# In every third attention step the next step's score products stand in front of the transposes

## The chip, the cores and the metric

The kernel runs on one core of one Trainium2 chip. The metric is device time in microseconds (us) of one execution. The engines are named as in the profile: PE is TensorE's matmul stream, PEld its weight loads, ACT is ScalarE, DVE is VectorE, POOL is GpSimd and SP the queue that issues most DMAs.

## The reference

The program computes an attention with a hash mask and then two dense feed-forward layers:

```
q_bits, k_bits = (q @ proj > 0), (k @ proj > 0)       # 6 bits per row
mask   = bucket(q_bits)[:, None] == bucket(k_bits)[None, :]
scores = where(mask, q @ k.T / sqrt(64), -1e9)
attn   = softmax(scores) ;  x = attn @ v               # 2 x 8 heads, 768 rows, 64 columns
x = (h * sigmoid(1.702 h)) @ w_out,  h = x @ w_in      # 1536 x 512, inner size 2048
y = (h * tanh(softplus(h))) @ w_out2, h = x @ w_in2
```

All inputs are float32. The kernel keeps that precision by splitting each operand into a high and a low part and adding three products.

## The kernel before, in words

Attention comes first, in one loop over steps `i` (line 821). There are 16 heads of 768 rows, and a step is 128 rows of one head, so 96 steps and a few more to drain. Three steps make a group, two groups (six steps) a head. In one step `i`, four kinds of work of different steps stand side by side:

- `qk(i + 1)` (letter Q, line 603): four products on PE of 384 columns each, which write the 128x768 scores of the next step into a PSUM tile `s`, of which there are two. The second two of them add the mask.
- `clamp(i)` (C, line 621) on DVE: the scores go from PSUM to SBUF, with the row's extreme. It is what frees the tile `s`. `expo(i)` (E, line 630) on ACT: the exponential with the row sum; it ends with a short instruction that reads the accumulator.
- `trp(g, t)` (A and B, line 673), twice in a step: three PE transposes put 128 columns of the three probability tiles of group `g` into one PSUM tile `pt`, and ACT casts that tile to `pth` (the high part). `trl` (a and b, line 686): DVE subtracts to get the low part `ptl`, which is the last reader of `pt`. Group `g` is worked on in steps `3g+3` to `3g+5`, so the first transposes of a group read the exponentials of the three steps just before, the last of them that of step `i - 1`.
- `pv` (P and R, line 693): four products with V of what was transposed in the step before, into the PSUM tile `u`. After the last of a group `u_out` (line 705) copies `u` to SBUF on ACT. This happens in the steps with `i % 3 == 0`, behind the exponential.

Letter T stands for the work listed by step in `todo`: loads, preparation of the next heads, normalisation, the first weights of the feed-forward layers. On PE it has two parts. `s2` (lines 501 and 489) computes hash logits with six products into a tile `prep`, at steps `i % 6 == 2`, and DVE reads that tile as `mk`. `norm1` (line 655) transposes row sums into such a tile, at steps `i % 12 == 5`. Both take their tile from the same pool as the transposes:

```
ps_t = es.enter_context(tc.tile_pool(name="ps_t", bufs=3, space=PSUM))   # line 360
ptile = ps_t.tile([P, 512], F32, tag="pt", name="pt")                    # line 674, in trp
pt = ps_t.tile([P, 512], F32, tag="pt", name="prep")                     # line 502, in s2
```

The pool has three tiles, taken in turn. Who takes one waits for the last reader of the tile taken three before: for a `trp` in step `i` that is mostly a subtraction of the step before.

The order in which a step's parts are issued is written by hand, as a string of these letters (line 753), and each engine runs its instructions in that order. The string before is the same for all steps but step 2:

```
ORDER = "ACaBbETQPR"
for op in ORDER if i != 2 else ORDER.replace("TQ", "QT"):    # line 836
```

The feed-forward layers follow (`moe`, line 873). They are about two thirds of the time and are not touched.

Of the kernel before, what the change touches and what calls it, by code (L numbers as in the profile page):

```python
# [41 lines left out]
def lsh_attention_moe_kernel(  # L42
# [291 lines left out]
    def r_in(m, f, k0=0, k1=KD):  # L334
        if k0 == 0:
            pool, tag = mps["h"], f"h{f % 2}"
            if (m, f // 2) == (0, 1):
                pool, tag = (mps["q"], "Y") if f % 2 else (mps["h"], "y0")
            h_t[m, f] = pool.tile([P, CH], F32, tag=tag, name="h")
        h = h_t[m, f]  # L340
        wh, wl = w_t[m, f, 0]
        n = 3 * k0
        for kk in range(k0, k1):
            wk = slice(kk * P, (kk + 1) * P)
            for a, x in ((wh, xr_hi), (wh, xr_lo), (wl, xr_hi)):
                nc.tensor.matmul(  # L346
                    h, a[:, wk], x[:, kk], start=(n == 0), stop=(n == 3 * KD - 1)
                )
                n += 1

    def attention():
        with ExitStack() as es:
# [67 lines left out]
            def keep_warm(n, cols):  # L420
                t = ps_t.tile([P, 512], F32, tag="pt", name="warm")
                for _ in range(n):
                    nc.tensor.matmul(t[:, :cols], ones[:, :P], ones[:, :cols], start=True, stop=True)
# [179 lines left out]
            def qk(i, parts=(0, 1), fs=(0, 1)):  # L603
                n, t = divmod(i, NT)
                kh, qx, qb, kb, _ = opnd[n]
                if 0 in parts and 0 in fs:
                    st_t[i] = ps_s.tile([P, 2, 512], F32, tag="s", name="s")
                s = st_t[i]
                c = slice(t * P, (t + 1) * P)
                both = (qx, kh, True), (qb, kb, False)  # L610
                for a, bb, st in [both[x] for x in parts]:
                    for f in fs:
                        nc.tensor.matmul(  # L613
                            s[:, f, :HS],
                            a[:, c],
                            bb[:, f * HS : (f + 1) * HS],
                            start=st,
                            stop=not st,
                        )

            def clamp(i):
                s = st_t[i]
                sb = pp.tile([P, 2, HS], F32, tag="p", name="p")
                mn = sm.tile([P, 1], F32, tag="mn", name="mn")
                nc.vector.tensor_scalar(  # L625
                    sb, s[:, :, :HS], NEG, None, ALU.min, ALU.min, accum_out=mn
                )
                st_t[i] = (sb, mn)

            def expo(i):  # L630
                sb, mn = st_t.pop(i)
                n, t = divmod(i, NT)
                p = sb.rearrange("p a b -> p (a b)")
                u, h = divmod(n, 2)
                if t == 0 and h == 0:
                    z_t[u] = sm.tile([P, 2 * NT], F32, tag="z", name="z", bufs=2)
                zc = NT * h + t
                nc.scalar.activation(  # L638
                    p,
                    p,  # L640
                    AF.Exp,
                    bias=mn,
                    scale=-1.0,
                    accum_out=z_t[u][:, zc : zc + 1],
                )
                p_t[i] = p
# [26 lines left out]
            def trp(g, t):  # L673
                ptile = ps_t.tile([P, 512], F32, tag="pt", name="pt")
                for j in range(3):
                    nc.tensor.transpose(  # L676
                        ptile[:, j * P : (j + 1) * P],
                        p_t[3 * g + j][:, t * P : (t + 1) * P],
                        ident,
                    )  # L680
                hi = ptp.tile([P, HS], F32R, tag="pth", name="pth")
                lo = ptp.tile([P, HS], F32R, tag="ptl", name="ptl")
                nc.scalar.copy(hi, ptile[:, :HS])  # L683
                pt_t[g, t] = (hi, lo, ptile)

            def trl(g, t):
                hi, lo, ptile = pt_t[g, t]
                nc.vector.tensor_sub(lo, ptile[:, :HS], rnd(hi))  # L688
                if t == NT - 1:
                    for j in range(3):  # L690
                        p_t.pop(3 * g + j)

            def pv(g, t):
                n, f = divmod(g, 2)
                hi, lo, _ = pt_t.pop((g, t))
                if t == 0:
                    u_t[g] = ps_u.tile([P, 512], F32, tag="u", name="u")
                ut = u_t[g]
                vv = opnd[n][4][0]
                nc.tensor.matmul(ut[:, :HS], vv[:, t, :], hi, start=(t == 0), stop=False)  # L700
                nc.tensor.matmul(ut[:, :HS], vv[:, t, :], lo, start=False, stop=(t == NT - 1))  # L701
                if t == NT - 1:
                    u_out(g)
# [47 lines left out]
            second[2]()  # L751
            LAG = 3
            ORDER = "ACaBbETQPR"
            NZ = 5
            NZL = 2
            PVLAG = LAG + 1
# [2 lines left out]
            def at(step, f, *args):  # L759
                todo.setdefault(step, []).append((f, args))  # L760
# [30 lines left out]
            for u in range(NHD // 2):  # L791
                zs = 2 * NT * (u + 1)
                nz = NZ if u < NHD // 2 - 1 else NZL
                at(zs + 1, norm0, u)
# [26 lines left out]
            for i in range(NSTEP + PVLAG):  # L821
                if i == NSTEP:
                    es_s.close()
                    mps["h"] = ctx.enter_context(
                        tc.tile_pool(name="ps_h", bufs=1, space=PSUM, side="right")
                    )
                parts = iter(range(max(0, 2 * (i - NSTEP)), min(2 * (i - NSTEP) + 2, 2 * KD)))
                for part in parts:
                    r_in(0, part // KD, part % KD, part % KD + 1)
                    break  # L830
                kk = i - LAG
                tr = 0 <= kk < NSTEP
                g, j = divmod(kk, 3)
                kv = i - PVLAG
                gv, jv = divmod(kv, 3)
                for op in ORDER if i != 2 else ORDER.replace("TQ", "QT"):
                    if op == "A" and tr:
                        trp(g, 2 * j)
                    elif op == "B" and tr:
                        trp(g, 2 * j + 1)  # L840
                    elif op == "a" and tr:
                        trl(g, 2 * j)
                    elif op == "b" and tr:
                        trl(g, 2 * j + 1)
                    elif op == "C" and i < NSTEP:
                        clamp(i)
                        if i == 3:
                            second[7]()
                    elif op == "E" and i < NSTEP:
                        expo(i)  # L850
                    elif op == "Q" and i + 1 < NSTEP:
                        qk(i + 1, (0, 1) if i else (1,))
                        if i == 0:
                            keep_warm(4, 256)
                    elif op == "P" and 0 <= kv < NSTEP:
                        pv(gv, 2 * jv)
                    elif op == "R" and 0 <= kv < NSTEP:
                        pv(gv, 2 * jv + 1)
                    elif op == "T":
                        while todo and min(todo) <= i:  # L860
                            st = min(todo)
                            f, args = todo[st].pop(0)
                            if not todo[st]:
                                del todo[st]
                            f(*args)
                for part in parts:
                    r_in(0, part // KD, part % KD, part % KD + 1)
# [5 lines left out]
    def moe():  # L873
        with ExitStack() as es:
# [354 lines left out]
            while due:  # L1229
                flush()  # L1230

    attention()
    moe()

# [53 lines left out]
```

## Time and profile before

| | us |
|---|---|
| median of 3 runs | 730.86 (730.52 to 731.77) |
| the profiled execution | 731.06 |
| its span, first to last instruction | 729.3 |
| PE busy | 723.5 (99%) |
| PEld busy | 631.5 (87%) |
| DVE busy | 616.3 (85%) |
| ACT busy | 469.0 (64%) |
| POOL busy | 185.4 (25%) |

The span is one execution, on the profiler's clock; the execution took 1.8 us more than its span. Busy times are sums over attention and feed-forward alike. PE's clock was granted in full nearly throughout (mean 0.999).

### The profile page before, as it was taken

How to read it: one execution, taken by the hardware profiler on the slowest of the kernel's cores; microseconds unless marked ns; L12 is line 12 of the kernel's file. 1: busy time of each engine (PE TensorE's matmuls, PEld its weight loads, DVE VectorE, ACT ScalarE, POOL GpSimd, SP SyncE). 2: the span in 40 equal slices, each digit the busy share in tenths (PEclk: the TensorE clock that was granted, in tenths of full speed). 3: DMA queues.
4: the chain of work that ended last, by engine and by line, in shares of the span. 5: the costliest groups of instructions: out<-in, count | busy, mean ns of one | idle time of the engine just before them, and what ended most of it. 6: DMA issues, size and time to landing. Idle time of an engine off the chain costs nothing.

```text
span 729.3 us, 11137 instructions
## 1 busy us (share of the span) xinstructions
PE 723.5 (99%) x3856; PEld 631.5 (87%) x3856; DVE 616.3 (85%) x1134; ACT 469.0 (64%) x957; POOL 185.4 (25%) x187
## 2 busy tenths in 40 slices
PE   8999999999999999999999999999999999999998
PEld 6999999999998788888888888888888888888886
DVE  8888889989888959878878797998699899897864
ACT  7888888888898765536546465576635656455340
POOL 7968877889893000000000000000000000000000
PEclk9999999999999999999999999999999999999999
DMA  5745656666624221121211221301302121211004
GB/s 157 199 125 145 190 141 163 182 157 153 170 85 118 109 70 48 58 87 64 82 58 58 88 88 60 112 0 59 115 0 87 59 75 69 88 58 58 1 1 173
DMA packets 25992, 69.53 MB, mean 95 GB/s; under 512 B 4464, under 2 KB 6992, under 8 KB 25936
## 3 DMA queue, kind: packets, MB, share of 16 engines
q1 hardware_dynamic: 25632, 68.62, 31.7%
q8 instruction: 30, 0.49, 0.3%
q10 hardware_dynamic: 304, 0.20, 0.1%
q14 instruction: 26, 0.21, 0.1%
HBM read 49.09 MB, written 3.19 MB: 72 GB/s over the span
## 4 chain that ended last, share of the span: by engine, by line
PE 94%; DVE 2%; ACT 2%; DMA 0%; issue 0%; DVEq 0%
PE y L947 36%; PE X L1010 11%; PE s L613 9%; PE pt L676 9%; PE Y L1010 8%; PE W L1010 7%; PE u L701 4%; PE u L700 4%; PE h L346 4%; PE prep L493 2%; ACT p L638 1%; DMA qn<-in_qt_dram 0%; ACT pth L683 0%; DVE gl L907 0%; DVE Y L1031 0%
## 5 line engine op out<-in xcount | busy, mean ns | idle before, releaser
L688 DVE TENSOR_TENSOR ptl<-pt,pth 128x384 fp32r<-128x384 f32 x192 | 98.1, 553 | 22.4 <-ACT pth L683 20.2
L683 ACT CAST pth<-pt 128x384 fp32r<-128x384 f32 x192 | 82.8, 484 | 28.7 <-PE pt L676 28.7
L638 ACT ACTIVATE p<-p,mn 128x768 f32<-128x768 f32 x96 | 91.2, 950 | 1.7 <-DVE p L625 1.6
L625 DVE TENSOR_SCALAR_CACHE_REDUCE p<-s 128x768 f32<-128x768 f32 x96 | 90.6, 945 | 0.3 <-PE s L613 0.2
L961 DVE TENSOR_TENSOR xq<-xq,y 128x512 f32<-128x512 f32 (+1 forms) x113 | 75.6, 679 | 13.7 <-PE y L947 13.0
L676 PE MATMUL pt<-ident,p 128*128 128x128 f32 x576 | 81.1, 274 | 0.1
L947 PE MATMUL y<-wh,gh 128*128 128x512 f32 (+1 forms) x194 | 75.4, 389 | 0.0
L947 PE MATMUL y<-wl,gh 128*128 128x512 f32 (+1 forms) x194 | 75.4, 389 | 0.0
L947 PE MATMUL y<-wh,gl 128*128 128x512 f32 (+1 forms) x194 | 75.2, 387 | 0.0
L947 PE MATMUL y<-gh,wh 128*128 128x512 f32 x192 | 75.0, 391 | 0.0
L947 PE MATMUL y<-gh,wl 128*128 128x512 f32 x192 | 74.9, 390 | 0.0
L947 PE MATMUL y<-gl,wh 128*128 128x512 f32 x192 | 74.7, 389 | 0.0
L259 ACT CAST wh<-wb 128x512 fp32r<-128x512 f32 x64 | 39.4, 620 | 54.5 <-DVE wb L246 26.2
L676 PEld LDWEIGHTS pt<-ident,p 128*128 128x128 f32 x576 | 68.5, 140 | 6.6 <-ACT p L638 2.4
L700 PE MATMUL u<-pth,vv 128*128 128x384 f32 x192 | 64.7, 337 | 0.0
L701 PE MATMUL u<-ptl,vv 128*128 128x384 f32 x192 | 64.5, 336 | 0.0
L613 PE MATMUL s<-kh,qx 128*128 128x384 f32 x192 | 55.7, 370 | 0.2 <-DVE p L625 0.2
L613 PE MATMUL s<-kb,qb 128*128 128x384 f32 x192 | 49.3, 337 | 0.3 <-POOL qk_m L473 0.2
L261 DVE TENSOR_TENSOR wl<-wb,wh 128x512 fp32r<-128x512 f32 x62 | 42.3, 687 | 3.9 <-ACT wh L259 3.6
L961 DVE TENSOR_TENSOR yr<-yr,y 128x512 f32<-128x512 f32 x56 | 38.2, 684 | 7.8 <-PE y L947 6.9
L947 PEld LDWEIGHTS y<-wh,gl 128*128 128x128 f32 x194 | 36.4, 188 | 7.6
L947 PEld LDWEIGHTS y<-wh,gh 128*128 128x128 f32 x194 | 36.5, 188 | 7.3 <-DVE xq L961 0.4
(272 smaller groups left out, 1842.1 us busy)
## 6 DMA issues: line engine op xcount, KB each, us to landing
raw<-in_wt_dram SPq DMA_DIRECT2D x64, 512.0 KB, 3.6
kn<-in_kt_dram SPq DMA_DIRECT2D x15, 384.0 KB, 4.2
vn<-in_vt_dram SPq DMA_DIRECT2D x8, 384.0 KB, 5.3
ul<-uh SPq DMA_DIRECT2D x16, 192.0 KB
rb<-scr SPq DMA_DIRECT2D x16, 192.0 KB, 3.5
qn<-in_qt_dram SPq DMA_DIRECT2D x15, 192.0 KB, 3.4
qx<-qk_m SPq DMA_DIRECT2D x15, 192.0 KB, 3.9
qb<-qk_m SPq DMA_DIRECT2D x15, 192.0 KB, 5.6
```

The costliest lines, as they stand in the source:

```text
L261: sub(lo, wf, rnd(hi))
L613: nc.tensor.matmul(s[:, f, :HS], a[:, c], bb[:, f * HS : (f + 1) * HS], start=st, stop=not st,)
L625: nc.vector.tensor_scalar(sb, s[:, :, :HS], NEG, None, ALU.min, ALU.min, accum_out=mn)
L638: nc.scalar.activation(p, p, AF.Exp, bias=mn, scale=-1.0, accum_out=z_t[u][:, zc : zc + 1],)
L676: nc.tensor.transpose(ptile[:, j * P : (j + 1) * P], p_t[3 * g + j][:, t * P : (t + 1) * P], ident,)
L683: nc.scalar.copy(hi, ptile[:, :HS])
L688: nc.vector.tensor_sub(lo, ptile[:, :HS], rnd(hi))
L700: nc.tensor.matmul(ut[:, :HS], vv[:, t, :], hi, start=(t == 0), stop=False)
L701: nc.tensor.matmul(ut[:, :HS], vv[:, t, :], lo, start=False, stop=(t == NT - 1))
L947: nc.tensor.matmul(y, w[:, js] if m == 0 else x[:, js], x if m == 0 else w[:, i0:i1], start=(n == 0), stop=(n == 5),)
L961: nc.vector.tensor_add(acc, acc, y)
L1010: nc.tensor.matmul(bk[b], w[:, k], x, start=(first and i == 0), stop=(hook is not None and i == 2), skip_group_check=True,)
```

## The change

In steps whose number divides by three, from step 3 on, letter Q moves from behind T to the front:

```
             ORDER = "ACaBbETQPR"
+            EARLY_Q = "QACaBbETPR"
...
-                for op in ORDER if i != 2 else ORDER.replace("TQ", "QT"):
+                for op in ORDER.replace("TQ", "QT") if i == 2 else ORDER if i % 3 or not i else EARLY_Q:
```

Q issues PE instructions alone: four weight loads and four products. In the 31 steps 3, 6, ..., 93 they come before the six transposes instead of behind them. From step 96 on there is no Q, and the two strings say the same. The order on ACT, DVE, POOL and SP is unchanged, and so are all tiles and pools.

## Rows read from the trace of the kernel before

**Rows 1.** Busy time by engine in the attention's steps; columns PE, PEld, DVE, ACT, POOL.
```profile
13.00:229.00 216.00, 215.91 (x1436) 208.50 (x1435) 193.49 (x409) 186.26 (x429) 176.21 (x168) 1.00 0.57 150
```

**Rows 2.** Waits of PEld in the same stretch: us in total, times, longest.
```profile
PEld pt L676 <- ACT p L638: 2.4, 10, 0.3
PEld s L613 <- DMA kb<-mk: 0.2, 1, 0.2
```

**Rows 3.** Timeline of PEld, steps 12 to 15: start, length, what, idle before.
```profile
32.17 0.31 PEld L676 LDWEIGHTS pt<-ident,p 128*128 128x128 f32 x2
32.72 0.42 PEld L676 LDWEIGHTS pt<-ident,p 128*128 128x128 f32 x4 [0.23 <-ACT p L638]
33.10 0.30 PEld L613 LDWEIGHTS s<-kh,qx 128*128 128x128 f32 x2
...
33.74 0.19 PEld L700 LDWEIGHTS u<-pth,vv 128*128 128x128 f32 x1
...
34.43 0.75 PEld L676 LDWEIGHTS pt<-ident,p 128*128 128x128 f32 x6
...
36.48 0.75 PEld L676 LDWEIGHTS pt<-ident,p 128*128 128x128 f32 x6
37.20 0.19 PEld L493 LDWEIGHTS prep<-qk_m,pwt 128*128 128x128 f32 x1
...
39.57 0.31 PEld L676 LDWEIGHTS pt<-ident,p 128*128 128x128 f32 x2
```

**Rows 4.** Timeline of ACT in steps 12, 13 and 15.
```profile
33.09 0.86 ACT L683 CAST pth<-pt 128x384 fp32r<-128x384 f32 x2 [0.42 <-PE pt L676]
33.84 0.94 ACT L638 ACTIVATE p<-p,mn 128x768 f32<-128x768 f32 x1
...
35.19 0.86 ACT L683 CAST pth<-pt 128x384 fp32r<-128x384 f32 x2
...
40.27 0.86 ACT L683 CAST pth<-pt 128x384 fp32r<-128x384 f32 x2 [1.25 <-PE pt L676]
```

**Rows 5.** Timeline of ACT from step 90 into 91, with no idle time between.
```profile
209.75 0.83 ACT L683 CAST pth<-pt 128x384 fp32r<-128x384 f32 x2
210.49 0.93 ACT L638 ACTIVATE p<-p,mn 128x768 f32<-128x768 f32 x1
...
211.42 0.45 ACT L712 COPY uh<-u 128x384 f32<-128x384 f32 x1
211.78 0.47 ACT L683 CAST pth<-pt 128x384 fp32r<-128x384 f32 x1
```

**Rows 6.** Timeline of DVE in steps 12 and 13.
```profile
33.60 1.02 DVE L688 TENSOR_TENSOR ptl<-pt,pth 128x384 fp32r<-128x384 f32 x2 [0.31 <-ACT pth L683]
34.54 0.95 DVE L625 TENSOR_SCALAR_CACHE_REDUCE p<-s 128x768 f32<-128x768 f32 x1
...
35.70 1.02 DVE L688 TENSOR_TENSOR ptl<-pt,pth 128x384 fp32r<-128x384 f32 x2 [0.21 <-ACT pth L683]
```

**Rows 7.** PE's sequencer waits at the `prep` products: whole stretch, then step 14.
```profile
L493 PEldq EVENT_SEMAPHORE  x14: 51/51/51, 23.2 to 199.3; - x14
...
L493 PEldq EVENT_SEMAPHORE  x1: 51/51/51, 36.8 to 36.8; - x1
```

**Rows 8.** Timeline of PEld, end of step 17 and start of 18.
```profile
44.38 0.09 PEld L657 LDWEIGHTS prep<-ident,z 128*12 128x12 f32 x1
...
45.84 0.83 PEld L676 LDWEIGHTS pt<-ident,p 128*128 128x128 f32 x6
```

**Rows 9.** Timeline of PEld and DVE, steps 3 and 4.
```profile
12.95 0.32 PEld L676 LDWEIGHTS pt<-ident,p 128*128 128x128 f32 x2
...
14.37 1.02 DVE L688 TENSOR_TENSOR ptl<-pt,pth 128x384 fp32r<-128x384 f32 x2 [0.37 <-ACT pth L683]
...
14.51 0.78 PEld L676 LDWEIGHTS pt<-ident,p 128*128 128x128 f32 x6
```

**Rows 10.** Timeline of PEld in step 96.
```profile
221.64 0.20 PEld L676 LDWEIGHTS pt<-ident,p 128*128 128x128 f32 x2 [0.24 <-ACT p L638]
```

## The prediction

> **What bounds the kernel now.** I first cut the busy times by stage: in the attention's steps PE is busy for 215.91 of 216.00 us, while DVE and ACT have 10 and 14% to spare [rows 1]. PE sets the pace there, so the time can change only by what PE waits for. The waits of its weight loads come next: only two kinds, 2.4 us in ten waits of the transposes for the exponential and one of 0.2 us for a DMA [rows 2]. Last I followed single steps on the timeline, on PEld, ACT and DVE, because what matters is which buffers come free when.
>
> A step on PE without a wait takes 2.05 us (34.43 to 36.48): six transposes, then the score products Q, then four V products of 0.69 together (33.74 to 34.43) [rows 3]. In step 12 the third transpose's load comes at 32.72, after 0.23 idle: it needs the exponential of step 11. Where six loads take 0.75 without a wait (36.48), the third stands some 0.29 behind the first, so at 32.46: it is 0.26 late. The next step starts at 34.43 instead of 34.22, so that costs PE 0.21; a load runs 0.05 ahead of its need, an estimate from these rows [rows 3]. Step 15 has no such wait: in front of it stand the six `prep` products, during which ACT catches up and then idles for 1.25 us [rows 4]. Step 18 has a small one (six loads in 0.83 instead of 0.75) because the `norm` transpose delays PE a little [rows 8, 3]. So only steps that begin a head (`i % 6 == 0`) wait, and step 3 and the last steps.
>
> **What it removes.** Of the ten waits nine lie in moved steps; the tenth is in step 96, where there is no Q [rows 2, 10]. That is 2.4 - 0.24 = 2.2 us. Seven smaller ones like step 18's (18, 30, ..., 90) give 0.08 each, 0.6 us. The Q products that go first wait for nothing new: they need the tile `s` that `clamp(i - 1)` frees, and DVE was at the next clamp by the start of the old step. The moved steps' T holds no PE work, and Q issues no DMA, so no queue is passed by another. Ceiling of the gain: 2.7 us.
>
> **What it delays.** In all 31 steps the transposes now start 0.69 later (four loads, as for the V products). ACT's cast follows, then DVE's subtraction, and that frees the `pt` tile. With three tiles the next taker waits for exactly this. How little room there is shows at `prep`: in all 14 of them PE's sequencer waits on a semaphore; in step 14 it does so at 36.8, just when the second subtraction of step 13 ends (35.70 + 1.02 = 36.72), and the load follows at 37.20 [rows 7, 6, 3]. The room is some 0.35 us. Now the chain in the new order, for the group that starts with step 12.
>
> - Q loads from 32.17, the first transpose at 32.86. The cast comes 0.70 after that load (39.57 to 40.27) [rows 3, 4], so at 33.56, 0.47 later than the 33.09 of before.
> - ACT then runs cast, cast, exponential, `uh` copy without a pause. From one pair of casts to the next that takes 2.03 where ACT was saturated (209.75 to 211.78) and 2.10 in step 12 itself (33.09 to 35.19) [rows 5, 4]. I take 2.05. The casts of step 13 start at 35.61, against 35.19; PE had its tile ready by 34.97, so ACT now binds.
> - The subtractions start 0.51 after the casts (35.19 to 35.70) and end 1.02 later [rows 4, 6]: 37.14. DVE has time: its clamp comes 0.94 after the first subtraction, 35.01, and a subtraction can follow it in 0.96.
> - `prep` can load some 0.11 later (0.04 to the sequencer, its 51 ns, and the start): 37.25.
> - PE without its wait is there at 32.17 + 2 x 2.05 + 0.72 (36.48 to 37.20) = 36.99 [rows 3]. It waits 0.26, of which 0.05 is hidden. A wait of 0.21 went and one of 0.21 came: net about 0.0 (+0.06 with 2.10).
>
> The first tile taken in step 13 that depends on step 12 is the fourth transpose's: subtraction 33.56 + 0.51 + 0.55, plus 0.05, is 34.67; PE asks at 34.21 + 0.39 = 34.60. That is 0.02 net, inside the chain above where a `prep` follows.
>
> The same chain, laid on the other groups:
>
> - Groups of 18, 30, ..., 78 (six): only 0.08 is saved; `prep` was at 45.84 + 0.08 + 4.10 + 0.72 = 50.74 and will be at 45.84 + 5.08 = 50.92, less 0.05: +0.14 each, +0.8 in all. Step 84, which hardly waited, the same: +0.2.
> - Groups of 15, 27, ..., 87 (seven), which saved nothing and end with `norm`: its load stood 44.38 - 39.57 = 4.81 after the start [rows 8, 3] and now stands at 37.14 - 32.17 + 0.05 = 5.02: less 0.05, +0.16 each, +1.1.
> - Groups of 9, 21, ..., 81 (seven), without either: the fourth transpose alone, +0.02 each, +0.1. Groups of 6, 12, ..., 72 (seven): 0 to +0.06 each, +0.1.
> - Step 3: no V products stand between it and step 4, so the tile is missed in full. Already before, step 4's loads took 0.78 instead of 0.75. The first transpose moves from 12.95 to 13.64, the subtraction from 14.37 to 14.34 + 0.51 = 14.85, so the fourth transpose of step 4 from 14.98 to 15.45 [rows 9]: +0.5.
> - Steps 90 and 93 save 0.4, but step 96 waits for the exponential of 95, and ACT has the same work in between [rows 10]: I keep -0.1 (bounds -0.4 and 0).
>
> Sum: 0.8 + 0.2 + 1.1 + 0.1 + 0.1 + 0.5 - 0.1 = +2.7 us. With 2.10 for ACT's turn it is 0.05 more in each of 21 chains: +3.8; with 2.03, +2.3. I take +3.2, between, because the copy also waits for its V products. The profiled execution took 731.06, so 734.3; the median of the runs lies 0.2 below it: **734.1**. The feed-forward part is one stream on PE and passes the shift on.
>
> The Trainium skill (Perfetto Trace Analysis, Optimization Strategy) says that a gap which repeats on the engine that should be saturated can mean too little PSUM for the next tile. Of the gaps of before that is not so, their row names the exponential; the rule speaks against this change, which makes the three tiles the place where PE waits. By it alone the old gaps would not move and the time would stay at 730.9.
>
> **The rivals.**
>
> 1. *The waits go and nothing takes their place: faster.* This holds if the tiles come free 0.25 us earlier than I reckon, so that the room at `prep` suffices; then 2.7 less the 0.3 that step 96 takes back: 728.5. For it: DVE and ACT have 10% to spare and waited for PE often. Against it: the turn with the copy is ACT's own length. Chance 0.12. The Trainium skill (Perfetto Trace Analysis, Matmuls) has groups rotate through PSUM banks so that their evacuation overlaps the next group's products; were it enough here, this would be the case.
> 2. *Only the direct miss remains.* The copy slips behind the next casts or ACT closes up by 0.2, and only the fourth transpose (31 x 0.02) and step 3 (0.5) pay, against 2.0 saved at heads (7 x 0.21 and 7 x 0.08): 730.86 - 2.0 + 0.6 + 0.5 - 0.1 = 729.9, up to no change where `prep` costs half. Chance 0.14, mostly within the bound below.
> 3. *The exponential is late again as well.* In my chain the exponential of step 14 or 17 ends 0.1 to 0.2 before the third transpose asks. If ACT loses 0.05 in each of three steps, 16 head starts wait up to 0.15 on top: +2.4, 736.5. Chance 0.14.
>
> **How the numbers follow.** Forecast 0.60, rivals 0.12, 0.14 and 0.14. A difference of 0.2% (1.5 us) is about what a measurement of this kernel can tell from none. Faster by more: rival 1 and little of 2, 0.13. Slower by more: the forecast without its lower edge, and rival 3: 0.72. Within: 0.15. The range 730.5 to 736.3 leaves out rival 1 and the far ends of 2 and 3.
>
> **What would show it.** In the changed profile the waits of the transposes for ACT's `p` should be gone but for step 96, and PEld should wait at L493, L657 and the fourth transposes for DVE's `ptl`. The `prep` load of step 14 should lie about 5.1 us behind the first load of step 12, and ACT should run from the casts of a moved step to those of the next without idle time. Step 4's fourth transpose should wait half a microsecond. Without waits at L493 the prediction is wrong.

## The result and the profile after

The changed kernel takes 735.71 us (median of six runs, 735.58 to 735.88), the kernel before 730.84 in the six runs beside it: a ratio of 1.0064, 95% interval 1.0051 to 1.0077. That is 4.9 us slower, where 3.2 were forecast. The profiled execution took 735.66 with a span of 733.8, against 731.06 and 729.3 before; the profile thus shows 4.5 us of the loss.

The waits of PE's weight loads in the attention come first, since PE has no other slack (it is busy for 219.49 of 220.00 us in that stretch of the changed kernel).

```profile
PEld u L700 <- ACT uh L712: 3.7, 24, 0.2
PEld pt L676 <- DVE ptl L688: 1.0, 2, 0.7
PEld u L700 <- issue: 0.4, 2, 0.2
PEld h L346 <- DVE p L625: 0.2, 1, 0.2
PEld u L700 <- POOL vv L109: 0.2, 1, 0.2
```

Columns: us in total, times, longest. Against [rows 2] the ten waits for the exponential `p` are gone, and no row of the list names it. In their place stand 24 waits of the first V product (L700) for `uh`, ACT's copy out of the tile `u`. No wait at `prep` is listed, though L493 was where it was expected: the list names no gap shorter than some 0.15 us, so the steps have to be read on the timeline. PEld in steps 12 to 14, the stretch of [rows 3]:

```profile
32.68 0.36 PEld L613 LDWEIGHTS s<-kh,qx 128*128 128x128 f32 x2
33.03 0.36 PEld L613 LDWEIGHTS s<-kb,qb 128*128 128x128 f32 x2
33.37 0.75 PEld L676 LDWEIGHTS pt<-ident,p 128*128 128x128 f32 x6
...
34.72 0.78 PEld L676 LDWEIGHTS pt<-ident,p 128*128 128x128 f32 x6
...
35.76 0.36 PEld L613 LDWEIGHTS s<-kb,qb 128*128 128x128 f32 x2
36.28 0.19 PEld L700 LDWEIGHTS u<-pth,vv 128*128 128x128 f32 x1 [0.15 <-ACT uh L712]
36.38 0.19 PEld L701 LDWEIGHTS u<-ptl,vv 128*128 128x128 f32 x1
...
36.92 0.75 PEld L676 LDWEIGHTS pt<-ident,p 128*128 128x128 f32 x6
37.78 0.19 PEld L493 LDWEIGHTS prep<-qk_m,pwt 128*128 128x128 f32 x1
...
40.17 0.36 PEld L613 LDWEIGHTS s<-kh,qx 128*128 128x128 f32 x2
```

Step 12's six loads take 0.75: the old wait is gone. Step 13 takes 2.20 (34.72 to 36.92) instead of 2.05. Of that 0.03 is the fourth transpose (0.78), and the V product stands 0.52 behind the start of the two loads in front of it (35.76 to 36.28), where 0.35 is usual (35.44 to 35.79 in the kernel before); the load after it follows 0.07 sooner than the usual 0.17, so 0.10 is left. In step 14 `prep` comes 0.86 behind the first transpose instead of 0.72 [rows 3], another 0.14. The `prep` load stands 37.78 - 32.68 = 5.10 behind the first load of the group, 0.28 later than 2 x 2.05 + 0.72 without waits. These are three small delays in one group, and they come from one chain, as ACT and DVE of the same steps show:

```profile
34.07 0.86 ACT L683 CAST pth<-pt 128x384 fp32r<-128x384 f32 x2 [0.85 <-PE pt L676]
34.83 0.94 ACT L638 ACTIVATE p<-p,mn 128x768 f32<-128x768 f32 x1
35.67 0.19 ACT L638 ACTIVATION_READ_ACCUMULATOR p<-p,mn 128x1 f32 x1
35.76 0.47 ACT L712 COPY uh<-u 128x384 f32<-128x384 f32 x1
36.12 0.87 ACT L683 CAST pth<-pt 128x384 fp32r<-128x384 f32 x2
...
34.59 1.02 DVE L688 TENSOR_TENSOR ptl<-pt,pth 128x384 fp32r<-128x384 f32 x2 [0.62 <-ACT pth L683]
35.52 0.95 DVE L625 TENSOR_SCALAR_CACHE_REDUCE p<-s 128x768 f32<-128x768 f32 x1
36.40 0.08 DVE L625 DVE_READ_ACCUMULATOR p<-s 128x1 f32 x1
36.64 1.02 DVE L688 TENSOR_TENSOR ptl<-pt,pth 128x384 fp32r<-128x384 f32 x2 [0.16 <-ACT pth L683]
```

ACT idles 0.85 before the late transposes, then runs casts, exponential, `uh` copy and the next casts without a pause. This stretch from one pair of casts to the next is called ACT's turn here: 34.07 to 36.12 is 2.05, the length of PE's own step, so the lateness is handed on in full. The copy ends at 36.23, and the V product that overwrites `u` loads at 36.28; the second subtraction ends at 37.66, and `prep` loads at 37.78.

The sum over a cycle of four groups can be read from PEld's loads, from the first load of a group to that of the next (first full cycle, groups of steps 12, 15, 18 and 21; the kernels other than these two are the experiments below):

| us | 12 (`prep`) | 15 (`norm`) | 18 (`prep`) | 21 (plain) | cycle |
|---|---|---|---|---|---|
| before | 7.39 | 6.27 | 7.26 | 6.14 | 27.06 |
| after | 7.49 | 6.48 | 7.49 | 6.29 | 27.75 |
| `only6` | 7.47 | 6.27 | 7.49 | 6.16 | 27.39 |
| `only63` | 7.53 | 6.48 | 7.34 | 6.29 | 27.64 |
| `half_all` | 7.18 | 6.27 | 7.18 | 6.14 | 26.77 |
| `a_qt` | 7.33 | 6.45 | 7.35 | 6.31 | 27.44 |
| `a_no_u` | 7.52 | 6.41 | 7.52 | 6.22 | 27.67 |
| `a_no_u_qt` | 7.27 | 6.33 | 7.29 | 6.23 | 27.12 |
| `a_no_copy` | 7.23 | 6.31 | 7.21 | 6.18 | 26.93 |

From the first `prep` load to the last, 13 heads, PEld takes 176.08 us before (23.66 to 199.74) and 179.94 after (23.93 to 203.87): 3.86 of the 4.5, or 0.59 a cycle. The first cycle's 0.69 is not typical, because of its group with `norm`: the other six such groups of the changed kernel take 6.41, 0.14 more than before. In the first one the V product loaded 0.11 behind the end of ACT's copy (43.72 to 43.83), in the others 0.05. Another 0.27 lies ahead of the first `prep` of these 13 heads and 0.37 behind the last. The 0.27 hides a difference that the change did not make: at the `prep` load of step 2, ahead of the first moved step, the changed kernel's profile was 0.29 earlier (11.62 against 11.91), and from there to step 8 it lost 0.56.

### The profile page after: what moved, and what is told of

The parts are those of the page before. It is cut to its first block, busy times and chain, and to the rows that moved or that the text cites. A ratio compares the mean times of both kernels' runs of the same rounds, so it can differ in the third digit from the quotient of the medians.

```text
span 733.8 us, 11146 instructions
## 1 busy us (share of the span) xinstructions
PE 728.2 (99%) x3856; PEld 630.4 (86%) x3856; DVE 613.1 (84%) x1134; ACT 464.8 (63%) x957; POOL 185.6 (25%) x187
## 4 chain that ended last, share of the span: by engine, by line
PE 95%; DVE 2%; ACT 1%; DMA 0%; issue 0%; SPq 0%; DVEq 0%
PE y L948 36%; PE X L1011 11%; PE s L613 9%; PE pt L676 9%; PE Y L1011 8%; PE W L1011 7%; PE u L700 5%; PE u L701 5%; PE h L346 4%; PE prep L493 2%; DMA qn<-in_qt_dram 0%; DVE gl L908 0%; DVE Y L1032 0%; DVE X L1032 0%; DVE qk_m L549 0%
## 5 line engine op out<-in xcount | busy, mean ns | idle before, releaser
L700 PE MATMUL u<-pth,vv 128*128 128x384 f32 x192 | 70.3, 366 | 0.0
L613 PE MATMUL s<-kh,qx 128*128 128x384 f32 x192 | 53.1, 357 | 0.3 <-DVE p L625 0.3
```

Source lines behind the costliest of these rows:

```text
L613: nc.tensor.matmul(s[:, f, :HS], a[:, c], bb[:, f * HS : (f + 1) * HS], start=st, stop=not st,)
```

## Experiments

The theory under test, theory 1: the transposes that start 0.69 later make ACT late, ACT makes DVE late, and the PSUM tiles that these two free (`u`, then the three `pt` tiles) make PE wait. Rivals: only the `pt` tiles matter (theory 2); or the moved products cost by themselves, whatever waits (theory 3). Every time below stands beside runs of the kernel before on the same chip, whose median there was 731.3 to 731.7; the expectations take it at 730.9, so differences are compared, not times.

**Cutting single waits.** The first four kernels take away what makes PE wait for `u`, for `pt`, and for both, the last of them without the change.

```
a_no_u:
-                nc.scalar.copy(uh[:, f * HS : (f + 1) * HS], ut[:, :HS])
+                nc.scalar.copy(uh[:, f * HS : (f + 1) * HS], rnd(hi))
a_no_pt:
-                nc.vector.tensor_sub(lo, ptile[:, :HS], rnd(hi))
+                nc.vector.tensor_sub(lo, rnd(hi), rnd(hi))
a_neither: both; b_neither: both, in the kernel before
```

> The changed kernel; the ACT copy of line 712 reads the high probability tile in SBUF instead of the PSUM tile u, so nothing has to leave u before the next group's first V product (the attention's output is left out of what follows). Theory 1 (the forecast of 3.2 us, completed: the single u tile is freed 0.5 us later and the first V product of each group waits for it, beside the pt tiles): the 24 waits at L700 are gone, groups without prep and norm lose their 0.13 each, groups with prep or norm keep their length because the subtraction of the step before sets it; 0.6 to 1.5 us less than the changed kernel, 734.2 to 735.1. Theory 2 (the pt tiles alone): no change against the changed kernel, 735.7. Theory 3 (the products cost more in their new place, whatever waits): 735.7.

Measured: 736.91 (ratio 1.0075, 1.0060 to 1.0090), no gain: theory 1 missed, and theories 2 and 3 had this total. The waits for `u` are gone, and others stand there:

```profile
PEld prep L493 <- issue: 2.5, 12, 0.2
PEld prep L657 <- DVE ptl L688: 1.1, 7, 0.2
PEld pt L676 <- DVE ptl L688: 0.9, 2, 0.7
...
PEld prep L493 <- POOL qx L477: 0.4, 2, 0.2
```

Now `prep` and `norm` take the whole wait, which was split between `u` and them. The timeline of PEld, steps 12 to 14 of this kernel:

```profile
32.73 0.36 PEld L613 LDWEIGHTS s<-kh,qx 128*128 128x128 f32 x2
...
36.16 0.19 PEld L700 LDWEIGHTS u<-pth,vv 128*128 128x128 f32 x1
...
36.85 0.79 PEld L676 LDWEIGHTS pt<-ident,p 128*128 128x128 f32 x6
37.86 0.19 PEld L493 LDWEIGHTS prep<-qk_m,pwt 128*128 128x128 f32 x1 [0.22 <-issue]
```

The `prep` load stands 5.13 behind the group's first, as late as before, since ACT and DVE are as late (a copy from SBUF takes 502 ns, one from `u` 469). Only plain groups, which have no second place to wait, got shorter: 6.29 to 6.22. Groups with `prep` got 0.03 longer, about what the copy from SBUF takes more, and groups with `norm` keep their length (6.41 to 6.43, against 6.41 in the changed kernel but for its first). So in groups with `prep` or `norm` the wait for `u` adds nothing; it only comes earlier than the other. Theory 2 does not hold even so, since without the wait for `u` the plain groups got shorter; theory 3 is decided below.

> The changed kernel; the DVE subtraction of line 688 reads the high tile twice instead of the PSUM tile pt, so a pt tile is free after ACT's cast (the low part of the probabilities is left out, it is zero). Theory 1: waits at prep, norm and the fourth transposes are gone, also the 0.5 us at step 4; the wait of the first V product for the u tile stays, 30 times some 0.1 to 0.15, against 2.5 us of old waits saved: 730.8 to 732.0. Theory 2: nothing is left to wait for, 728.5. Theory 3: 735.7.

> The changed kernel with both edits together (low part of the probabilities and the attention's output left out). Theories 1 and 2: all new waits are gone and the old ones for the exponential too, 2.4 to 2.7 us below the same two edits in the kernel before, 728.2 to 728.6. Theory 3: 4.9 us above them.

> The kernel before with both edits together (low part of the probabilities and the attention's output left out): the control. In it neither tile was waited for, so all theories expect the time of the kernel before within 0.3 us, 730.6 to 731.1, and the ten waits for the exponential unchanged at 2.4 us.

Measured: 793.28, 793.05 and 794.48 (ratios 1.0837, 1.0854 and 1.0873): all three missed by 60 us, by a cost that the edit brought in. The subtraction, now with both operands in SBUF, is no longer the same instruction in time (the subtractions of `a_no_pt`: count, then ns as least/median/most):

```profile
L688 DVE TENSOR_TENSOR ptl<-pth x152: 542/852/2242, 15.3 to 232.6; 128x384 fp32r<-128x384 f32 x152
```

In the changed kernel it is 540/548/559. These kernels say nothing of the `pt` tiles. The last pair differs by the moved products alone, and the one with them is 1.4 faster; with such large other waits around them that is a weak hint against the third theory, no more.

**Moving part of the steps.**

```
 only6:   ... else ORDER if i % 6 or not i else EARLY_Q    # 6, 12, 18, ...
 only63:  ... else ORDER if i % 6 != 3 else EARLY_Q        # 3, 9, 15, ...
```

> The changed kernel with the products moved only in the steps that begin a head (6, 12, ..., 90), the ones in which the transposes waited for the exponential. Theory 1 (the shift makes ACT, then DVE, late by half a microsecond, and PE meets a tile not yet free, u, pt at the fourth transposes, prep, somewhere in the group): these groups pay what they pay in the changed kernel, +0.1 (steps 12, 24, ...) and +0.2 (steps 18, 30, ...), no start-up cost: 2 to 2.8 us above the kernel before, 733. Rival: the cost lies in the steps that had no wait to fill (3, 9, 15, ...), and these steps alone give the gain of 2.2 us: 728.7.

Measured: 733.95 (1.0037, 1.0022 to 1.0051), +2.5: as expected. In the table, groups of 15 and 21 keep their old length (within 0.02); 12 and 18 have that of the changed kernel.

> The products moved only in steps 3, 9, 15, ..., 93, which had no wait to fill. Theory 1: step 4 pays 0.5; in the groups the transposes are late, ACT runs late to the end of the group and the next head's first transposes, which here stand in front of the products, wait for its exponential longer than before: the waits for p at the heads grow from 2.2 us to 5 or 6 in all; 734 to 735. Rival (cost at the tiles only): the heads' waits stay as they were, 0.2 per group with norm and 0.15 without plus 0.5, 733.5.

Measured: 735.56 (1.0059, 1.0044 to 1.0074), +4.1: at the upper edge. Groups 15 and 21 now have the length of the changed kernel, and the old waits grew, since the groups before the heads end later, but to 4.0 and not to the 5 or 6 expected:

```profile
PEld pt L676 <- ACT p L638: 4.0, 14, 0.4
PEld u L700 <- ACT uh L712: 1.9, 12, 0.2
```

The two halves sum to 6.6, the whole change costs 4.9. The difference of 1.7 fits the 1.6 by which these waits had grown (2.4 to 4.0) and which moving at the heads too saves.

**Half the delay.** Only the first two of the four products go in front; the two that add the mask stay behind the transposes, which thus start two loads later, not four.

```
-            EARLY_Q = "QACaBbETPR"
+            EARLY_Q = "qACaBbETrPR"
+                    elif op in "qr" and i + 1 < NSTEP:
+                        qk(i + 1, (0,) if op == "q" else (1,))
```

> In the same 31 steps only the first two of the four products (those without the mask) stand in front, the two of the mask stay behind T: the transposes are 0.35 later, of which 0.26 or 0.1 was waiting anyhow. Theory 1: the shift is within the room of the tiles (0.35 at prep), so most old waits go and little comes: 1.5 to 2.2 us faster than the kernel before, 728.7 to 729.4. Rival (each product in front costs by itself, in proportion): half of the change's 4.9, +2.4, 733.3.

Measured: 729.75 (0.9979, 0.9969 to 0.9988), 1.7 faster than the kernel before, as expected. PEld in step 12 and up to `prep`, of this kernel:

```profile
31.97 0.36 PEld L613 LDWEIGHTS s<-kh,qx 128*128 128x128 f32 x2
32.32 0.75 PEld L676 LDWEIGHTS pt<-ident,p 128*128 128x128 f32 x6
33.04 0.30 PEld L613 LDWEIGHTS s<-kb,qb 128*128 128x128 f32 x2
...
34.02 0.75 PEld L676 LDWEIGHTS pt<-ident,p 128*128 128x128 f32 x6
...
35.37 0.19 PEld L700 LDWEIGHTS u<-pth,vv 128*128 128x128 f32 x1
...
36.06 0.75 PEld L676 LDWEIGHTS pt<-ident,p 128*128 128x128 f32 x6
36.78 0.19 PEld L493 LDWEIGHTS prep<-qk_m,pwt 128*128 128x128 f32 x1
```

In this stretch no place waits: the exponential of the step before is in time, step 13 takes 2.04, and `prep` follows 0.72 behind. So 0.35 of delay fits into the room of ACT's chain and 0.69 does not. This also refutes theory 3, that products cost by themselves in front of transposes: step 12 takes 2.05 here, with two of them in front, and 2.04 in the changed kernel, with all four. The same from step 6 on, to spare step 4 its wait:

```
 ... ORDER if i % 3 or i < 6 else EARLY_Q
```

> Two of the four products in front in steps 6, 9, ..., 93, step 3 as before. Theory 1: the 1.7 us of the same edit with step 3, and 0 to 0.3 us more because step 4 does not wait for the pt tile: 1.7 to 2.1 us below the kernel before, 728.8 to 729.2 where that takes 730.9. Rival (gain of the start only): no difference from the kernel before.

Measured: 730.07 (0.9979, 0.9970 to 0.9988): the same ratio. The extra gain does not show, but 0 to 0.3 us is less than the interval of some 0.7 us to either side can tell. These two are the best kernels found; nothing separates them.

**Giving `prep` and `norm` more time.** In steps with `i % 6 == 2` and `i % 12 == 5` letter Q goes in front of T.

```
 ... ORDER.replace("TQ", "QT") if i == 2 or i % 6 == 2 or i % 12 == 5 else ...
```

> The changed kernel, and in the steps with prep or norm on PE (i % 6 == 2 and i % 12 == 5) the products stand in front of T, so that prep and norm ask for their pt tile 0.69 later. Theory 1: their waits for the subtraction of the step before go (0.1 to 0.2 in 22 groups), those for u and at the fourth transposes stay: 1.4 to 2.4 us below the changed kernel, 733.3 to 734.3. Rival (u alone, prep and norm wait for nothing): as the changed kernel, 735.7.

Measured: 734.66 (1.0043, 1.0028 to 1.0058), +3.2, so 1.7 below the changed kernel: as expected. The groups with `prep` get 0.14 to 0.16 shorter; those with `norm` gain nothing (6.39 to 6.41 from the second on, against 6.41), so for them only the total was right. The 24 waits for `u` stay (3.8 us). So of the 0.31 by which a group with `prep` is longer than the 7.18 without a wait, half is at `prep` itself and half in front of it.

> The changed kernel with both cures at once: prep and norm behind the products, and the ACT copy reading the high probability tile instead of u (the attention's output is left out of what follows). Theory 1 (three tiles share one late chain, so a wait cured alone moves to the next tile): now only the fourth transposes (30 times 0.03 to 0.05) and step 4 (0.5) pay, against 2.4 us saved; 730.0 to 731.5 on a chip where the kernel before takes 730.9, that is -0.9 to +0.6 against the kernel before. Rival (what is left at L700 was the whole price, prep and norm being apart): the sum of the two cures taken alone, 0 for the copy and 1.7 for the order: 734.0, +3.1.

Measured: 733.60 (1.0034, 1.0022 to 1.0047), +2.3: missed by both, the theory and its rival. The profile has waits beside the chain, among them 1.9 us for the DMA that brings the mask:

```profile
PEld pt L676 <- DVE ptl L688: 2.0, 5, 0.7
PEld s L613 <- DMA kb<-mk: 1.1, 1, 1.1
PEld s L613 <- DMA qb<-mk: 0.8, 1, 0.8
```

Why the mask was late is open: the profile of the change once more, below, has such a wait of 0.9 too, that of `half_from6` two, and that of `a_qt`, with the same order, none. So the total decides nothing. But the cycle of the table lies ahead of these waits (the first comes at 168.93). There the two cures alone save 0.08 and 0.31 against the changed kernel and both together 0.63, more than their sum, which speaks for theory 1: a wait cured alone moves to the next tile. What is left, 0.35 above the 26.77 of `half_all`, is about twice what was expected, since in groups with `prep` the fourth transpose now waits in both steps (2.08 for step 13; in step 14 it loads 0.48 behind the first, not 0.39).

**The root.** With ACT's turn of 2.05 as long as PE's step, nothing of the lateness is caught up. Taking the `uh` copy off ACT shortens the turn and leaves PE's order as in the changed kernel. It also unties `u`, which nothing reads any more; but `a_no_u` had untied `u` and kept the turn long, and the loss stayed. So what separates this kernel from `a_no_u` is the turn (and a fill on POOL).

```
-                nc.scalar.copy(uh[:, f * HS : (f + 1) * HS], ut[:, :HS])
+                nc.gpsimd.memset(uh[:, f * HS : (f + 1) * HS], 0.5)
```

> The changed kernel without the ACT copy of u: POOL fills the tile with 0.5 instead, out of the way (the attention's output is left out of what follows). Theory 1 (the shift of the transposes is not absorbed because ACT's turn with the copy, 2.05 us, is as long as PE's step): without it ACT's turn is 1.67 us, ACT catches up within a step, the waits at L700, prep and norm all go, the fourth transposes of the steps after a moved one (30 times 0.03) and step 4 (0.5) remain, against 2.4 us saved; 0.5 to 1.5 us below the kernel before. Rival (the tiles are late by DVE's own turn or by the shift alone): the waits at prep and norm stay as in the run that only cut the tie to u, 3 to 5 us above the kernel before.

Measured: 731.15 (0.9991, 0.9980 to 1.0001), 0.6 below the kernel before and by the interval hardly to be told from it: the lower edge of what was expected. The loss of the change is gone; the rival's +3 to +5 did not come. ACT in steps 12 and 13 of this kernel:

```profile
34.59 0.86 ACT L683 CAST pth<-pt 128x384 fp32r<-128x384 f32 x2 [0.90 <-PE pt L676]
35.34 0.94 ACT L638 ACTIVATE p<-p,mn 128x768 f32<-128x768 f32 x1
36.18 0.19 ACT L638 ACTIVATION_READ_ACCUMULATOR p<-p,mn 128x1 f32 x1
36.27 0.85 ACT L683 CAST pth<-pt 128x384 fp32r<-128x384 f32 x2
```

The turn is 1.68, and the waits at `u`, `prep` and `norm` all vanish: `prep` loads 0.72 behind the first transpose of step 14 again, not 0.86 as in the changed kernel or 1.01 as in `a_no_u`. What is left of the cost (26.93 against 26.77 a cycle) is 0.03 to 0.05 a group, the fourth transposes: they miss the first step's subtraction directly, before any catching up.

**The change once more**, beside new runs of the kernel before.

> The changed kernel once more, as the reference on this chip: 4.5 to 5.2 us above the kernel before, 735.4 to 736.1 where that takes 730.9.

Measured: 736.28 (1.0069, 1.0055 to 1.0082), +4.9: as expected.

## Why the prediction was right, and where its size was off

Direction and mechanism held; the size was 1.7 us short (3.2 forecast, 4.9 measured), though the time lies inside the range.

- *The waits that go.* Groups 12 and 18 without any wait are 7.18 (`half_all`): 0.21 and 0.08 below the kernel before, the two figures of the forecast. In the changed kernel the waits for `p` are gone, even in step 96, where one was expected to stay; there PE now waits 0.25 for DVE at L346 instead. Rival 3, the exponential late again, did not come, and neither did rival 2: ACT closed up nowhere, its turn was 2.05 in 28 of the 30 moved steps that have the copy.
- *The chain.* `prep` behind the first load of step 12: 5.08 forecast, 5.10 measured. ACT's turn: 2.05 forecast and measured. `norm` behind the start of its group: 5.02 forecast, 5.03 or 5.04 measured in all seven. `a_no_copy` beside `a_no_u` shows that the turn is the cause, and with it why rival 1 (nothing takes the waits' place) failed: it asked for tiles 0.25 earlier.
- *Step 4.* PEld in steps 3 and 4 of the changed kernel:

```profile
12.66 0.36 PEld L613 LDWEIGHTS s<-kh,qx 128*128 128x128 f32 x2
...
13.35 1.08 PEld L676 LDWEIGHTS pt<-ident,p 128*128 128x128 f32 x9
15.18 0.31 PEld L676 LDWEIGHTS pt<-ident,p 128*128 128x128 f32 x3 [0.74 <-DVE ptl L688]
```

  The fourth transpose stands 15.18 - 12.66 = 2.52 behind the first load of step 3, forecast 2.50 (15.45 - 12.95), where it was 2.03 before [rows 9]: the +0.5.
- *First wrong term: "It waits 0.26, of which 0.05 is hidden".* At `prep` nothing is hidden. In the kernel without waits the second load of `prep` already follows the first by 0.11 (36.78, then 36.89), and in the changed kernel by the same 0.11 (37.78 to 37.89): the 0.05 had been read at the transposes and carried over to a place where it does not hold. A group with `prep` costs 0.30 instead of 0.21 (the rest is 0.02 from the longer chain and 0.02 behind `prep`). In a cycle that is 2 x 0.09 = 0.18. For `norm`, where the forecast took off the same 0.05, the term held: 0.14 against 0.16. PEld in step 29 of the changed kernel, the end of its second group with `norm`:

```profile
72.13 0.75 PEld L676 LDWEIGHTS pt<-ident,p 128*128 128x128 f32 x6
72.93 0.08 PEld L657 LDWEIGHTS prep<-ident,z 128*12 128x12 f32 x1
72.95 0.30 PEld L613 LDWEIGHTS s<-kh,qx 128*128 128x128 f32 x2
...
74.31 0.36 PEld L613 LDWEIGHTS s<-kh,qx 128*128 128x128 f32 x2
```

  `norm` loads 0.80 behind the first transpose instead of 0.72, but the next step follows 1.38 behind it (72.93 to 74.31), not 1.46 (44.38 to 45.84) [rows 8]. So 0.08 of the wait is hidden here, and the group pays its 0.14 a step earlier, at the fourth transpose and at `u`.
- *Second wrong term: "Groups of 9, 21, ..., 81, without either: the fourth transpose alone, +0.02 each".* They grew by 0.15. The prediction followed the three `pt` tiles and overlooked the single tile `u` (pool `ps_u`, line 361, `bufs=1`), which the same late ACT frees with its copy. It could have been worked out from the trace of before, steps 12 and 13:

```profile
34.80 0.48 ACT L712 COPY uh<-u 128x384 f32<-128x384 f32 x1
...
35.44 0.36 PEld L613 LDWEIGHTS s<-kb,qb 128*128 128x128 f32 x2
35.79 0.19 PEld L700 LDWEIGHTS u<-pth,vv 128*128 128x128 f32 x1
```

  There the copy ended at 35.28, 3.11 behind the group's start, and the first V product loaded at 35.79, 3.62 behind it; without the old wait 3.41. A copy 0.47 later ends at 3.58, past 3.41. In a cycle that is 0.13, from the plain group; in the others the wait for `u` only comes first, as `a_no_u` shows, and takes part of the wait that was announced for L493. "Without waits at L493 the prediction is wrong" was thus too strict a test: the list shows none, the timeline shows 0.14.

The forecast had 0.0 + 0.16 + 0.14 + 0.02 = 0.32 a cycle (its 0.14 for the group of 18 is 0.13 by its own figures, which changes nothing in its sum). With 0.18 and 0.13 for the two wrong terms and 0.02 less for `norm` that is 0.61; over the 13 heads the mean was 0.59. This is 0.27 a cycle more than forecast and 1.8 in all: the 2.7 of the sum with a turn of 2.05 and these 1.8 are the profile's 4.5. Counted from step 2, where the changed kernel's profile was 0.29 ahead, the loss is 4.8; the 0.3 more lie mostly in the last steps, where step 91 took 2.27 (2.06 before) and PE waited at L346. The 0.5 that the forecast put on top for a longer turn has no counterpart in the trace, where the turn is 2.05; by luck it covered a part of what was missed.

The Trainium skill (Perfetto Trace Analysis, Optimization Strategy) says that a gap that keeps recurring on the engine that should be saturated can mean too little PSUM for the next tile. Here the trace agrees for the new gap (24 waits of 0.15 at a single tile), and `a_no_u` shows its limit: without that wait the time stayed (736.91), because the next tile in the same chain made PE wait instead. That more PSUM would have helped is not shown.

What stays open: how much each `pt` tile costs with ACT unchanged, since `a_no_pt` brought its own cost; a second `u` or a fourth `pt` tile was not tried. In `half_all` three heads of its profile take 13.57 to 14.01 instead of the 13.32 to 13.48 of the others. In each of them DVE runs an instruction for the feed-forward weights (steps 48, 60 and 74; L238, L243, L238), which took 0.99, 1.15 and 1.88 us there, against 0.91, 0.68 and 0.48 in the changed kernel; why it takes now more and now less is open.

## What to carry to other kernels

When work is moved in front of an engine's stage, follow its lateness through every tile that the delayed engines free, single ones first, and not only through the pool that already looks tight. Compare the turn of the helping engine with the step of the bounding one: where they are equal (2.05 and 2.05 here) nothing is caught up, and a wait cut at one tile can reappear at the next. If a move cures one wait and makes another, try half of it: two products in front instead of four gained 1.7 of the 2.7 us that the forecast had as the ceiling.

## What the runs showed of the hardware that was not expected

- The subtraction on DVE took 548 ns (median) with one operand in PSUM and 852, up to 2242, with both in SBUF (`a_no_pt`, to 233 us), while POOL's operations beside it grew too: the one at L481 from 1841 to 1984 ns on average, at L582 from 1017 to 1188, the one at L109 that writes `kh` from 843 to 1114. The slow ones are those that overlap with POOL. Of all 192 subtractions of `a_no_pt` 60 overlapped no POOL instruction and took 542 to 559 ns; 132 overlapped one and took 546 to 2709, median 1174. In the changed kernel 169 overlapped one and took 540 to 559. The kernel took 62 us longer than the kernel before, 57 more than the change alone. The Trainium skill (SBUF — State Buffer, Who interferes with whom) states that a DVE instruction with two SBUF inputs contends with a GpSimd instruction that reads SBUF, for a shared read interface; the trace agrees.
- A wait of PE is partly hidden in some places and not in others: the load after the waiting one follows 0.10 behind instead of 0.17 at L700, 0.03 instead of 0.11 at `norm` (L657), but by 0.11 with and without a wait at `prep`.
